# One long order for attention, soft experts and top-1 expert: phase 1 re-ordered, the tail cut into single operations, the guess taken from five experts, eight banks in one pool

## The chip, the cores and the metric

The kernel runs on one core of a Trainium2 chip. The metric is device time in microseconds (us) of a whole execution. Times are medians of runs; a profiled execution, of which the profiler keeps every instruction, is read for the reasons.

The engines are TensorE (PE, products; PEld its weight loads), VectorE (DVE), ScalarE (ACT), GpSimd (POOL) and SyncE (SP), which here only issues DMAs. Each works off its own queue in order. TensorE writes into eight PSUM banks of 128 x 512 floats; VectorE and ScalarE evict them.

## The reference

Three layers follow one another on 4608 tokens of 512 features (8 batches of 576 tokens, 8 heads of 64):

```
q_s = softmax(q, over the head's 64 features)          # per token and head
k_s = softmax(k, over the 576 tokens)                  # per feature
x   = q_s @ (k_s^T @ v)                                # attention without a score matrix

logits = x @ phi                                       # 4608 x 32, 8 experts of 4 slots
d = softmax(logits, over all tokens);  slot_input = d^T @ x
slot_out[e] = relu(slot_input[e] @ w1[e]) @ w2[e]      # 8 experts, 512 -> 1024 -> 512
x = softmax(logits, over the 32 slots) @ slot_out      # "combine"

logits2 = x @ w_gate;  e = argmax;  gate = softmax(logits2)[e] * sigmoid(x @ w_output_gate)[e]
out = gate * (relu(x @ w1_2[e]) @ w2_2[e])             # top-1 expert, 512 -> 1024 -> 512
```

All data is float32. The inputs are 28.3 MB of q, k and v, 33.6 MB of weights for the soft experts and 4.2 MB for each expert of the third layer.

## The kernel before

**Phase 1** runs over eight units `u` (a pair of batches and half of the heads each). A unit's k, q and v are loaded by `lk`, `lq`, `lv` (lines 182 to 195). On k: a maximum (`kmax`, L205), an exponential with its sum in quarters (`kexp`, L213), transposes (`ktr`, L223) and their evictions (`kev`), products with v (`kv`, L248), and the small matrices made from them. On q, in two parts: maximum (`qmax`, L318), subtraction on GpSimd (`qsub`), exponential (`qexp`), sum (`qsum`, L336, with an added epsilon and a reciprocal), multiplication on GpSimd (`qmul`), transposes (`qtr`, L357), evictions (`qev`). An eviction goes through `evac` (L199 on ScalarE for the letter `A`, L201 on VectorE for `D`). Logits come from `lg` (L377). Per pair of units an online softmax over tokens follows (`lmax` to `sc`): `su` (L419) collects slot inputs, and `sc` (L505, L506) adds them into `acc` and their denominator into `den`.

The string `ORDER` names each of these operations with its bank or home (`ktr.0.0:L1`, `kev.0.4:A,eT0`); a loop calls them in that order, and under a manual schedule each engine's queue is filled in just that order. It is the result of a search by a planner. Weights of the soft experts come in 32 pieces of 1 MB (`lw.0` to `lw.31`, four per expert: two of `w1`, two of `w2`). There are 19 homes in the on-chip memory, shared with k, q and v; `W_HOMES` gives the home of each piece. `ORDER` holds `lw.0` to `lw.16`; the others are issued by `reload` as soon as a home's last user has been called.

**The tail** has its own pools of banks (three `tp`, two `kv`, two `L`, one `U`), taken after phase 1's pool is closed (L599). It begins with the combine softmax over `l_all` (`combine_soft`, L567 to L577), the division of `acc` by `den` (L636 to L638), a transpose (L640) and its copy `sT` (L643). `SEQ` orders what follows: `i`/`j` an expert's first products (`expert_in`, L675; experts 0 to 5 do both halves in one paired pass), `t` its hidden rows transposed (L693), `o`/`p` the second products (L710), `c` a ninth of the combine weights split and transposed into `cstack` (L616, L626, L629), `m`, `d`, `n`, `r` means, distances and radii of the combine weights per batch, `G` the guess (L837 to L865): after seven experts the first token is put through the sum of these experts (`so_g`) and `w_gate`, the argmax is read into a register of SP, and that expert's weights of the third layer are loaded in eight pieces (L863, L865).

`SEQ2` orders the routing. As every token's row of x is a mix of the same 32 rows of slot outputs, a hidden unit of the guessed expert mostly has one sign for all tokens. `prep_a` and `prep_b` (L1246, L1257) form the units' values, `units` (L1259) tests each against the radii, `pack` (L1298) ranks the units that are not certain (at most 128 are kept) and selects them, `rows` (L1323) computes their row numbers and gathers their rows of `w2` by an indirect DMA (L1335) into `w2u`, `slots` (L1344) forms their mixing weights `smix`; certain units that are on are summed into one 32-row matrix `ml` (`linear_out` L1363, `linear_sum` L1371). `wsplit` (L1355, L1356) splits the gathered rows into two parts `wmh`, `wml`. `route`, `l2_tiles` (L940) and `gating` compute the second routing.

The output loop (L1427) runs over 12 groups of 3 tiles of 128 tokens. Per group `relu_part` (L1405, L1409, L1410) makes hidden rows in two parts `his`, `los`; per tile four products (L1437 with `ml`, three of L1439) and an eviction scaled by `gates` (L1442 on ScalarE, L1444 on VectorE); stores go out on SP (L1416). Groups 5 and 6 also count tokens that went to other experts (`count`, `others`); a loop over these experts (L1465) computes them with the whole 1024-unit network. It runs zero times when the guess holds for all tokens and the kept units suffice.

## Time and profile before

| | |
|---|---|
| median of 3 runs | 260.06 us (260.02 to 261.18) |
| the profiled execution | 261.23 us |
| its span, first to last instruction | 259.4 us |
| TensorE busy / VectorE / ScalarE / GpSimd | 218.4 / 157.5 / 125.5 / 93.7 us |
| mean granted clock of TensorE | 0.915 of full speed |
| read from memory / written | 66.42 / 9.44 MB |

Busy times are sums over the span; they say little of a single stage, so the rows below go by stage. The granted clock has two levels, 1.00 (2.4 GHz) and 0.50 (1.2 GHz); a mean between them is a mix of the two in time.

### The profile page before, as it was taken

How to read it: one execution, taken by the hardware profiler on the slowest of the kernel's cores; microseconds unless marked ns; L12 is line 12 of the kernel's file. 1: busy time of each engine (PE TensorE's matmuls, PEld its weight loads, DVE VectorE, ACT ScalarE, POOL GpSimd, SP SyncE). 2: the span in 40 equal slices, each digit the busy share in tenths (PEclk: the TensorE clock that was granted, in tenths of full speed). 3: DMA queues.
4: the chain of work that ended last, by engine and by line, in shares of the span. 5: the costliest groups of instructions: out<-in, count | busy, mean ns of one | idle time of the engine just before them, and what ended most of it. 6: DMA issues, size and time to landing. Idle time of an engine off the chain costs nothing. (4 is left out here: it accounts for less than half of the span.)

```text
span 259.4 us, 6248 instructions
## 1 busy us (share of the span) xinstructions
PE 218.4 (84%) x2497; PEld 155.7 (60%) x2497; DVE 157.5 (61%) x315; ACT 125.5 (48%) x276; POOL 93.7 (36%) x102
## 2 busy tenths in 40 slices
PE   0397989998999999998399997998788869999940
PEld 0285777687887777774244451574675448887830
DVE  1989898979988795623675345223631075768430
ACT  0748989889998877533110211242300134553410
POOL 4268597962797987400100532001114002000000
PEclk9999999999999999999779997999955558999995
DMA  7999999999999999799719899938501003674780
GB/s 257 400 422 388 401 366 417 373 415 365 386 311 418 417 416 413 299 418 326 282 38 414 355 423 418 410 117 350 238 0 40 0 3 121 282 286 169 303 303 9
DMA packets 13203, 76.34 MB, mean 294 GB/s; under 512 B 1712, under 2 KB 3120, under 8 KB 6128
## 3 DMA queue, kind: packets, MB, share of 16 engines
q1 hardware_dynamic: 12800, 75.50, 73.8%
q8 instruction: 23, 0.38, 0.6%
q0 software_dynamic: 80, 0.26, 0.4%
q10 hardware_dynamic: 288, 0.10, 0.2%
q14 instruction: 12, 0.10, 0.1%
HBM read 66.42 MB, written 9.44 MB: 292 GB/s over the span
## 5 line engine op out<-in xcount | busy, mean ns | idle before, releaser
L349 POOL TENSOR_TENSOR qt<-qt,qi 128x1280 f32<-128x1280 f32 (+1 forms) x14 | 29.7, 2119 | 13.3 <-DVE qi L342 5.0
L325 POOL TENSOR_TENSOR qt<-qt,qm 128x1280 f32<-128x1280 f32 (+1 forms) x14 | 29.5, 2120 | 8.3 <-DVE qm L318 8.0
L248 PE MATMUL kv<-ek,vt 128*64 128x64 f32 x512 | 21.3, 231 | 0.6 <-DMA vt<-in_v_dram 0.6
L248 PEld LDWEIGHTS kv<-ek,vt 128*64 128x64 f32 x512 | 18.3, 144 | 3.2 <-issue 2.2
L336 DVE TENSOR_REDUCE qs<-qt 128x20 f32<-128x1280 f32 (+1 forms) x14 | 18.7, 1334 | 0.6 <-ACT qt L329 0.6
L318 DVE TENSOR_REDUCE qm<-qt 128x20 f32<-128x1280 f32 (+1 forms) x14 | 18.5, 1333 | 0.0
L675 PE MATMUL kv<-we,sT 128*32 128x256 f32 (+1 forms) x288 | 16.9, 357 | 0.0
L329 ACT ACTIVATE qt<-qt 128x1280 f32<-128x1280 f32 (+1 forms) x14 | 16.4, 1169 | 1.0 <-POOL qt L325 1.0
L213 ACT ACTIVATE kt<-kt,km 128x576 f32<-128x576 f32 x20 | 15.4, 774 | 2.3 <-DVE km L205 2.3
L205 DVE TENSOR_REDUCE km<-kt 128x4 f32<-128x2304 f32 x5 | 12.7, 2532 | 4.6 <-DMA kt<-in_k_dram 4.6
L199 ACT COPY ek<-p 128x512 f32<-128x512 f32 (+1 forms) x25 | 13.1, 555 | 3.7 <-PE p L223 3.6
L223 PE MATMUL p<-ident,kt 128*128 128x128 f32 x70 | 12.5, 311 | 1.9 <-ACT ksum L269 0.8
L710 PE MATMUL U<-we,hte 128*32 128x512 f32 x88 | 12.3, 670 | 1.8 <-DVE hte L695 1.8
L357 PE MATMUL p<-ident,qt 128*128 128x128 f32 x88 | 13.2, 280 | 0.6 <-POOL qt L349 0.4
L1439 PE MATMUL kv<-mst,hr 128*128 128x512 f32 (+1 forms) x30 | 12.1, 405 | 0.7 <-ACT hr L1409 0.7
L199 ACT COPY eT<-p 128x512 f32<-128x512 f32 (+1 forms) x21 | 10.8, 532 | 3.8 <-PE p L357 3.6
L675 PEld LDWEIGHTS kv<-we,sT 128*32 128x32 f32 x288 | 9.3, 116 | 5.6 <-issue 2.4
L223 PE MATMUL L<-ident,kt 128*128 128x128 f32 x20 | 3.8, 313 | 10.4 <-ACT kt L213 9.9
L629 ACT CAST cstack<-tp 128x512 fp32r<-128x512 f32 x9 | 5.3, 587 | 14.7 <-PE tp L626 14.7
L1439 PE MATMUL L<-mst,hr 128*128 128x512 f32 (+1 forms) x30 | 11.9, 399 | 0.0
L223 PEld LDWEIGHTS p<-ident,kt 128*128 128x128 f32 x70 | 8.7, 156 | 4.7 <-ACT kt L213 1.4
L357 PEld LDWEIGHTS p<-ident,qt 128*128 128x128 f32 x88 | 9.6, 140 | 3.1 <-issue 1.9
(331 smaller groups left out, 523.1 us busy)
## 6 DMA issues: line engine op xcount, KB each, us to landing
we<-in_w_dram SPq DMA_DIRECT2D x26, 1024.0 KB, 8.6
out_dram<-ob SPq DMA_DIRECT2D x11, 768.0 KB, 3.3
...
```

The lines of the kernel that those rows point to most:

```text
L199: nc.scalar.copy(out=o, in_=i)
L213: nc.scalar.activation(out=t, in_=t, func=AF.Exp, bias=st_["km", u][:, x:x + 1], accum_out=st_["ksum", u][:, x:x + 1])
L223: nc.tensor.transpose(t[:, n * P:(n + 1) * P], ks_[u][:, j * P:(j + 1) * P], ident)
L248: nc.tensor.matmul(o[D * hh:D * hh + D, x * D:x * D + D], va, ek[:, g:g + D], start=(j == js[0]), stop=(j == js[-1]))
L318: nc.vector.tensor_reduce(out=m[:, :n], in_=t.rearrange("p (x d) -> p x d", d=D), op=ALU.max, axis=AX.X)
L325: nc.gpsimd.tensor_tensor(out=t, in0=t, in1=m.unsqueeze(2).to_broadcast([P, n, D]), op=ALU.subtract)
L329: nc.scalar.activation(out=t, in_=t, func=AF.Exp)
L336: nc.vector.tensor_reduce(out=s[:, :r, :HH], in_=t.rearrange("p (r h d) -> p r h d", h=HH, d=D), op=ALU.add, axis=AX.X)
L349: nc.gpsimd.tensor_tensor(out=t, in0=t, in1=s.unsqueeze(2).to_broadcast([P, n, D]), op=ALU.mult)
L357: nc.tensor.transpose(t[:, n * P:(n + 1) * P], qs_[u][:, o:o + P], ident)
L675: nc.tensor.matmul(hp[NS * g:NS * g + NS, o], sT[:, c, :], w, start=(c == 0), stop=(c == C - 1))
L1439: nc.tensor.matmul(op, a[:, x], w[:, d0:d1], start=False, stop=(k == 2))
```

## The change

Phase 1 has a new `ORDER` from a new search; the tail's functions are cut into named single operations too, and one string `TAIL` (with a short `LAST` behind it) gives their order, their banks, and for evictions their engine. Much of the diff is that cutting. What differs in the work:

- Unit 0's k is loaded in four pieces and its q in two, and `kmax` of unit 0 works by quarters.
- `qsum` is cut into `qsum`, `qadd` and `qrec` (the same three instructions).
- 19 weight pieces are issued in `ORDER`; `lw.19` to `lw.31` stand in `TAIL` by hand instead of through `reload`.
- One pool of eight banks (`p0 p1 p2 kv0 kv1 L0 L1 U`) serves both phases.
- `acc` is transposed without being divided by `den`; the reciprocal `rd` scales each expert's hidden rows when they are evicted (`hc`).
- The guess is made from five experts (`EG = 5`), and the other three accumulate in a bank of their own.
- Twelve dummy products (`h.n:bank` does n) stand at four places of `TAIL`.
- The units' test scales the batch means by the inverse root of the radii (a power on GpSimd) and takes a minimum over the eight batches before it squares; the selection is made by four instructions per half instead of one.
- The first products of five tiles (`AHEAD`) stand ahead of `LAST`, which holds the split of the gathered rows.
- The last stores go out on the queue of the engine that evicted them.

```
-SEQ = """i0 j0 i1 j1 t0 i2 j2 m0 o0 p0 c t1 i3 j3 m1 o1 p1 c f t2 d0 d1 i4 j4 c o2 p2 m2 t3 n0 n1 d2 d3 i5 j5 c o3 p3 t4 n2 n3
-r0 c o4 r1 p4 t5 r2 i6 j6 c o5 p5 t6 c o6 p6 G0 c G1 G2 G3 i7 c j7 c t7 c o7 p7"""
-SEQ2 = """
-a.0 a.1 b.0 a.2 b.1 u0.0 a.3 b.2 q.0 b.3 k.0 u0.1 u0.2 u1.0 r.0 l.0 k.1 r.1 u1.1 u1.2 s.0 s.1 c.0 u0.3 u1.3 g.1 4.0
-l.1 4.1 g.2 c.1 5.0 g.3 w.0 g.4
-"""
+LOOP = "kv0 L0 U kv1 L1".split()
+AHEAD = 5
+ORDER = """
+lk.0.0:k0 lq.0.0:k1 lk.0.3 lq.0.1 lk.0.1 lk.0.2 lk.1:k2 lq.1:k3 lv.0:x0 lv.1:x1 lk.3:q0 lq.2:q1 lk.2:eq0 lq.5:eq1
+kmax.0.0 kexp.0.0 qmax.0.0 ktr.0.0:p0 kev.0.0:A,eT0 kmax.0.3 qsub.0.0 qmax.0.1 kexp.0.3 ktr.0.4:p1 kmax.0.1 kev.0.4:A
...
+TAIL = """
+cs.0 xt:p0 hz.1 hz.0 zc.0 xc:A zc.2 h.4:L0 in.0:p1 rc.0 xr.0 cs.1 zc.1 xr.1 zc.3 in.2:p2 cs.2 lw.19 lw.20 hc.0:D zc.4
+zc.5 zc.6 cs.3 tr.0:L1 lw.21 lw.22 in.1:kv0 hc.2:A hr.0:D cs.4 cs.5 cs.6 o.0.0:kv1 hc.1:A in.3:U lw.23 ca.0 ft.0 me.0
...
+o.1.1 ds.3.3 lw.28 lw.29 nm.3.0 ds.2.2 nm.3.1 ct.3:L1 nm.3.2 hz.3 nm.2.0 ds.2.3 o.2.0 cc.3:D ca.5 cd.5 ct.2:p0 lw.30
+nm.2.1 ct.5:p1 nm.2.2 ca.4 cc.2:D tr.3:U tr.4:p2 cc.5:A cd.4 o.2.1 hc.5:A hr.3:D ra.0 ca.7 i.6:L1 cd.7 lw.31 hz.4
+hr.4:D o.3.0 o.3.1 j.6 hz.5 o.4.0 hc.6:D o.4.1 tr.6:p0 G.0 hz.6 ct.4:p1 hr.6:D tr.5:U G.1:kv0 ca.6 cc.4:D hr.5:A cd.6
+ct.7:p2 G.2 G.3:L1 cc.7:D ct.6:kv1 G.4 o.5.0:p0 cc.6:D ca.8 cd.8 i.7:U G.5 zc.7 o.5.1 zc.8 zc.9 zc.10 ct.8:p1 hz.7
+o.6.0 cc.8:D j.7 o.6.1 hc.7:D G.6 tr.7:kv0 ra.1:p2 hr.7:A ra.2 h.2:L0 o.7.0 ra.3 lm.0 lm.1 lm.2 lm.3 ln.0 ln.1 ln.2
+ln.3 ra.4:kv1 ra.5 o.7.1 ra.6 rc.2 sb.0 sb.1 h.5:L0 to.0:L1 zc.11 to.1 tc.0:D q.0:p1 tc.1:D h.1:L0 q.3 a.0:U q.1 q.2
+a.1:kv0 ac.0:D l.1.0:p2 ac.1:D l.0.0:kv1 b.0:p0 a.2:L1 a.3:p1 ac.2:D b.1 ac.3:D b.2:U u.0.0 u.0.1 l.0.1 u.0.8 u.0.2
+u.0.7 u.0.4 b.3 u.0.3 u.0.9 u.0.5 l.0.2 u.0.6 u.1.7 k.1.0:kv0 u.0.10 u.1.1 u.1.8 k.0.1:L1 u.0.11 u.1.0 u.1.2 l.0.3
+u.1.9 u.1.4 k.0.2 4.0:p1 k.0.3 k.0.4 k.0.5 k.0.6 u.1.3 l.0.4 u.1.5 u.1.6 s.0:p0 u.1.10 l.0.5 u.1.11 k.1.1 rw.0:U
+lc.0:D k.1.2 k.1.6 4.1 k.1.3 k.1.4 k.1.5 ga.0.0 ga.0.1 ga.0.2 rw.1 5.0:A ga.0.3 l.1.1 ga.0.4 rw.2 5.1:L1 ga.0.9 rw.3
+ga.0.5 ga.0.11 l.1.2 ga.0.13 ga.0.6 5.2 s.1 ga.0.7 l.1.3 5.3 s.2 l.1.4 ga.0.8 rl.0:kv1 rl.1:kv0 ga.0.10 l.1.5 rh.0
+ga.0.12
+"""
+LAST = """
+ga.0.14 lc.1:A rz.0 ga.0.15 w.0 rh.1 w.1 rz.1
+"""
...
-    def kmax(u):
-        m = sp.tile([P, 4], F32, tag="km", name="km", bufs=2)
+    def kmax(u, x=None):
...
+        o = slice(0, 4) if x is None else slice(x, x + 1)
         nc.vector.tensor_reduce(
-            out=m, in_=ks_[u].rearrange("p (x s) -> p x s", x=4), op=ALU.max, axis=AX.X, negate=True
+            out=st_["km", u][:, o], in_=ks_[u].rearrange("p (x s) -> p x s", x=4)[:, o], op=ALU.max, axis=AX.X,
+            negate=True,
         )
...
+    def hot(n, bk):
+        scratch = bank(bk)
         for _ in range(n):
             nc.tensor.matmul(scratch[:, :4 * VC], zero[:, :P], zero, start=True, stop=True)
...
-    nc.vector.tensor_scalar(out=acc, in0=acc, scalar1=rd, scalar2=None, op0=ALU.mult)
-    ts_ = bank("tp")
-    nc.tensor.transpose(ts_[:, :P], acc, ident)
+    def xt(bk):
+        t = bank(bk)
+        nc.tensor.transpose(t[:, :P], acc, ident)
+        sx["xt"] = t
...
+    def hc(e, eng):
+        t = sp.tile([P, FQ], F32, tag="pm", name="h_sb", bufs=3)
+        scaled(eng, t, sx.pop(("hp", e))[:, :FQ], rd)
+        sx["h", e] = t
...
+    EG = 5
...
+    def e_out(e, j, bk=None):
+        if bk:
+            sx["so", e // EG] = bank(bk)
...
+                start=(e in (0, EG) and j == 0),
+                stop=(e in (EG - 1, E - 1) and j == 1),
...
+            nc.gpsimd.tensor_tensor(out=rsq, in0=rsq, in1=mhalf, op=ALU.pow)
...
+        elif x == 3:
+            nc.vector.tensor_reduce(out=vmn[:, ks], in_=v, op=ALU.min, axis=AX.X)
...
+        elif x == 6:
+            nc.vector.tensor_tensor(out=unf[:, ks], in0=vmn[:, ks], in1=asq[:, ks], op=ALU.is_le)
...
+        else:
+            i = k0 + x - 3
+            nc.vector.tensor_scalar(
+                out=KX["gu"][:, i], in0=io1, scalar1=rkk[:, i:i + 1], scalar2=None, op0=ALU.is_equal
+            )
...
+    early = {i: bank(m) for i, m in enumerate(LOOP[:AHEAD])}
+    for i, t in early.items():
+        nc.tensor.matmul(t, cstack[:, i * P:(i + 1) * P], ml, start=True, stop=False)
+    do(LAST)
...
-                op = bank(m_tags[n % 5])[:, :d1 - d0]
+                op = early.get(i)
                 x = slice(t * P, (t + 1) * P)
-                nc.tensor.matmul(op, cstack[:, i * P:(i + 1) * P], ml[:, d0:d1], start=True, stop=False)
+                if op is None:
+                    op = bank(LOOP[n % len(LOOP)])[:, :d1 - d0]
+                    nc.tensor.matmul(op, cstack[:, i * P:(i + 1) * P], ml[:, d0:d1], start=True, stop=False)
...
-                    store_all(g, t, t + 1, d0, d1)
+                    store_all(g, t, t + 1, d0, d1, nc.scalar if eng == "A" else nc.sync)
```

In `TAIL`, `cs` is the combine softmax, `xt`/`xc`/`xr` the transpose, its copy and the reciprocal, `in`/`i`/`j` the experts' first products, `hc` their eviction, `tr`/`hr` transpose and rectifier, `o` the second products, `ca`/`cd`/`ct`/`cc` the combine weights, `G` the guess, `lm`/`ln` its loads, `sb`/`to`/`tc` the sum of the two banks of experts with transpose and copy, `q`/`l`/`lc`/`ga` the second routing, `a`/`ac`/`b`/`u` the units, `k` ranks and selection, `rw` row numbers and gather, `s` mixing weights, `4`/`5` the linear part, `w` the split of the gathered rows, `rl`/`rh`/`rz` the hidden rows of a group.

## Rows read from the trace of the kernel before

**Rows 1.** The page's strip of 40 slices: what the transfers moved.

```profile
GB/s 257 400 422 388 401 366 417 373 415 365 386 311 418 417 416 413 299 418 326 282 38 414 355 423 418 410 117 350 238 0 40 0 3 121 282 286 169 303 303 9
```

**Rows 2.** By stage: length, busy PE, PEld, DVE, ACT, POOL, clock, DMA share, GB/s.

```profile
9.87:104.00 94.13, 89.15 (x1350) 70.88 (x1352) 83.07 (x116) 80.05 (x175) 70.64 (x45) 1.00 1.00 393
104.00:126.30 22.30, 20.06 (x304) 14.20 (x300) 8.36 (x21) 8.35 (x23) 3.20 (x6) 1.00 0.88 338
...
130.70:177.30 46.60, 44.12 (x532) 21.30 (x533) 20.22 (x58) 9.93 (x24) 9.92 (x24) 0.93 0.79 317
177.30:188.20 10.90, 8.65 (x84) 6.24 (x81) 6.23 (x29) 3.48 (x12) 0.68 (x1) 1.00 0.72 290
188.20:208.70 20.50, 16.68 (x72) 11.29 (x71) 4.45 (x14) 1.66 (x4) 3.93 (x7) 0.50 0.04 13
208.70:215.40 6.70, 5.44 (x11) 3.71 (x12) 4.34 (x12) 2.50 (x6) 0.23 (x1) 0.50 0.01 2
```

**Rows 3.** The timeline at the handover: start, duration, engine, line, what; in brackets idle before.

```profile
125.90 0.35 DVE L505 SCALAR_TENSOR_TENSOR acc<-acc,w,L 128x128 f32<-128x128 f32 x1 [1.10 <-PE L L496]
...
129.34 0.28 DVE L638 TENSOR_SCALAR acc<-acc,rd 128x128 f32<-128x128 f32 x1
...
130.69 0.20 PEld L675 LDWEIGHTS kv<-we,sT 128*32 128x32 f32 x8 [0.53 <-ACT sT L643]
```

**Rows 4.** TensorE's timeline in the experts, and where it leaves them.

```profile
139.60 0.44 PE L693 MATMUL tp<-ident,h_sb 128*128 128x128 f32 x2
139.97 1.93 PE L675 MATMUL kv<-we,sT 128*32 128x256 f32 x32
...
142.25 1.92 PE L710 MATMUL U<-we,hte 128*32 128x512 f32 x16
...
146.65 0.66 PE L626 MATMUL tp<-ident,st 128*128 128x128 f32 x4
...
177.25 0.40 PE L585 MATMUL tp<-zero 128*128 128x264 bf16 x2
```

**Rows 5.** The timeline of the gather, its split, and the first output product.

```profile
193.80 1.21 POOL L1335 DMA_INDIRECT kx<-in_m2r_dram,idx  x1 [7.50 <-DVE idx L1334]
...
208.76 0.80 PE L1437 MATMUL kv<-mst,cstack 128*128 128x512 f32 x1 [0.76 <-DVE mst L1373]
...
209.19 0.60 ACT L1355 CAST mst<-kx 128x512 fp32r<-128x512 f32 x1
...
209.82 0.69 DVE L1356 TENSOR_TENSOR mst<-kx,mst 128x512 fp32r<-128x512 f32 x1
...
kx<-in_m2r_dram,idx POOLq DMA_INDIRECT x1, 3.6
```

**Rows 6.** The timeline of the output loop: two groups' hidden rows, and the last eviction.

```profile
216.83 0.34 PE L1405 MATMUL tp<-cstack,kx 128*128 128x384 f32 x1
...
219.77 0.33 PE L1405 MATMUL tp<-cstack,kx 128*128 128x384 f32 x1
...
249.43 0.48 DVE L1444 TENSOR_SCALAR ob<-L,gates 128x256 f32<-128x256 f32 x1 [0.20 <-PE L L1439]
```

**Rows 7.** The timeline at the start of phase 1.

```profile
6.31 2.55 DVE L205 TENSOR_REDUCE km<-kt 128x4 f32<-128x2304 f32 x1 [4.64 <-DMA kt<-in_k_dram]
6.36 1.28 ACT L213 ACT_TABLE_LOAD   x1 [6.36 <-DMA kt<-in_k_dram]
...
9.87 0.44 PE L223 MATMUL L<-ident,kt 128*128 128x128 f32 x1 [9.87 <-ACT kt L213]
```

**Rows 8.** VectorE's groups by line, 9.87 to 104 us: busy, mean ns, idle before.

```profile
L201 DVE COPY ek<-p 128x512 f32<-128x512 f32 x5 | 3.5, 692 | 1.7 <-PE p L223 1.7
```

**Rows 9.** The stores' line by itself: duration of an issue on SP, min/median/max in ns.

```profile
L1416 SPq DMA_DIRECT2D out_dram<-ob x15: 332/332/580, 216.9 to 250.5; - x15
```

**Rows 10.** SP's timeline: the last weight pieces and the guess's loads.

```profile
149.60 4.23 SPq L547 DMA_DIRECT2D we<-in_w_dram  x6
172.74 2.18 SPq L863 DMA_DIRECT2D vz<-in_m_dram  x4
```

More of the change, by code (lines that the diff above doesn't have):

```diff
@@ L893, in tile_attention_soft_moe_top1_moe @@
-    x = 0
-    for op in SEQ.split():
-        if op == "c":
-            combine(x)
-            x += 1
-        else:
-            steps[op[0]](*map(int, op[1:]))
-    warm(WARM[0])
-    so_sb = sp.tile([P, DM], F32, tag="U_sb", name="so_sb")
-    so7 = st_e.pop("so7")
-    for i in range(2):
-        o = slice(i * DM // 2, (i + 1) * DM // 2)
-        nc.vector.tensor_tensor(out=so_sb[:, o], in0=so7[:, o], in1=so_g[:, o], op=ALU.add)
-    cstack = st_["cstack"]
-    tso = bank("tp")
-    for c in range(C):
-        nc.tensor.matmul(
-            tso[:, c * P:(c + 1) * P], so_sb[:, c * P:(c + 1) * P], sum4.rearrange("p c s -> p (c s)"),
-            start=True, stop=True,
-        )
@@ new lines, in tile_attention_soft_moe_top1_moe, with sb, to @@
+    so_b = sp.tile([P, DM], F32, tag="so_b", name="so_b")
+    soT = sp.tile([P, C, P], F32, tag="kvT", name="soT")
+    HM = DM // 2
+    def sb(x):
+        o = slice(x * HM, (x + 1) * HM)
+        nc.vector.tensor_tensor(out=so_b[:, o], in0=sx["so", 1][:, o], in1=so_g[:, o], op=ALU.add)
+    def to(x, bk=None):
+        if bk:
+            sx["to"] = bank(bk)
+        for c in range(2 * x, 2 * x + 2):
+            nc.tensor.matmul(
+                sx["to"][:, c * P:(c + 1) * P], so_b[:, c * P:(c + 1) * P], sum4.rearrange("p c s -> p (c s)"),
+                start=True, stop=True,
+            )
@@ new lines, in tc_, with q_ @@
+    def tc_(x, eng):
+        evac(eng, soT[:, 2 * x:2 * x + 2], sx["to"][:, x * HM:(x + 1) * HM].rearrange("p (c x) -> p c x", c=2))
+    gst = late.tile([P, 2 * E], F32R, name="gst")
+    l2 = late.tile([P, NT, 2 * E], F32, name="l2")
+    def q_(x, bk=None):
+        if x in (0, 3):
+            t = sx["q"] = bank(bk) if bk else sx["q"]
+            for c in (0, 1) if x == 0 else (2, 3):
+                nc.tensor.matmul(t[:, :2 * E], soT[:, c, :], wgo[:, c, :], start=(c == 0), stop=(c == C - 1))
+        elif x == 1:
+            nc.scalar.copy(out=gst, in_=sx["q"][:, :2 * E])
+        else:
+            nc.vector.tensor_tensor(
+                out=gst[64:], in0=sx.pop("q")[64:, :2 * E], in1=gst[64:].bitcast(F32), op=ALU.subtract
+            )
@@ L980, in prep_a @@
         def prep_a(j):
[L981 removed]
+            s4 = cbank("L")
             for c in range(C):
@@ L1344, in slots @@
[L1344 to L1360 removed]
+                    r[:, i:KH], ones, unf[:, k0 + i - 1:k0 + i].to_broadcast([P, KH - i]), start=False,
@@ new lines, in s_, with w_ @@
+    def s_(x, bk=None):
+        if bk:
+            sx["s"] = bank(bk)
+        if x < 2:
+            for i in range(KH * x, KH * x + KH):
+                nc.tensor.matmul(
+                    sx["s"][:, :P], KX["tma"][:, i, 0:P], KX["gu"][:, i], start=(i == 0), stop=(i == KF - 1)
+                )
+        else:
+            nc.scalar.copy(out=KX["smix"], in_=sx.pop("s")[:, :P])
+    def w_(x):
+        if x == 0:
+            nc.scalar.copy(out=KX["wmh"], in_=KX["w2u"])
+        else:
+            nc.vector.tensor_tensor(out=KX["wml"], in0=KX["w2u"], in1=KX["wmh"].bitcast(F32), op=ALU.subtract)
@@ L1361, in linear_out, with lo_ @@
+    def lo_(h, bk=None):
+        if bk:
+            sx["m"] = bank(bk)
         for kk in range(KH * h, KH * h + KH):
@@ new lines, in tile_attention_soft_moe_top1_moe, with rl, rh @@
+    his, los, obs, hps = {}, {}, {}, {}
+    def rl(g, bk=None):
+        W = GT * P
+        t = hps[g] = bank(bk) if bk else cbank("tp")
+        nc.tensor.matmul(t[:, :W], KX["smix"], cs_[0][:, g * W:(g + 1) * W], start=True, stop=True)
+    def rh(g):
+        W = GT * P
+        if not his:
+            KX.update(hr=home("eT0", "hr", F32R), lr=home("eT1", "lr", F32R))
+        o = (g % 6) * W
+        his[g] = KX["hr"][:, o:o + W]
+        los[g] = KX["lr"][:, o:o + W]
+        nc.scalar.activation(out=his[g], in_=hps[g][:, :W], func=AF.Relu)
```

1046 lines of the change are left out of this document (517 added, 529 removed).

## The prediction

> **What bounds the kernel now.** I read the strip of 40 slices first [rows 1], then busy time by stage [rows 2], then the timeline at each place where one stage hands over to the next. TensorE is the engine to follow, and its share means something else in each stage. From the first transpose to 104 us it is busy 89.15 of 94.13 us at a granted clock of 1.00 (2.4 GHz), VectorE 83.07 and ScalarE 80.05: three engines near full, so an order can only win what lies idle. From 130.7 to 177.3 us (the eight experts) it is busy 44.12 of 46.6 us at a mean clock of 0.93 [rows 2]; the weights stream meanwhile, after a hole in which the transfers stood still (the slices at 38 and, later, 117 GB/s [rows 1]). From 188.2 to 215.4 us the clock is 0.50 (1.2 GHz) [rows 2]: latency chains with small products, and the first tiles of the output loop at half speed. That gives five terms: A phase 1, B the handover to the experts, C the experts, D routing up to the first output product, E the loop. Their boundaries are 126.25 us (last accumulation of the state, 125.90+0.35), 130.69 (first expert product) [rows 3], 177.25 (TensorE leaves the last expert for dummy products) [rows 4], 208.76 (first output product) [rows 5] and 249.43 (last eviction begins) [rows 6].
>
> **A, phase 1 (126.25 us now).** Unit 0's k and q are now loaded in pieces, and k's maximum is taken by quarters. Before, VectorE starts at 6.31 us, when all of k has landed, and reduces for 2.55; the table load (1.28) runs beside it; the first transpose comes at 9.87 [rows 7]. A quarter of 1152 KB at some 400 GB/s [rows 1] lands 2.2 us earlier (0.7 instead of 2.9) and is reduced in 0.64 us, so the table load becomes the longer arm: it ends at 6.31-2.2+1.28 = 5.4 us, and with the 1.0 us that lay between the end of the reduction (8.86) and the first transpose, TensorE starts at 6.4 us, 3.5 sooner [rows 7]. The added reductions are the old 2.55 us cut up; the four added loads take SP 0.33 to 0.58 us each in its queue [rows 9], ahead of data that needs 0.7 us a piece. Splitting the denominators into named steps adds no instruction. The rest is a permutation: every product stays, but by the letters of the two orders ten evictions go from ScalarE to VectorE (88 and 24 become 78 and 34), at 0.69 us [rows 8] 6.9 us more for VectorE, which has 11.1 us idle up to 104; most of the new ones stand in the last units, where it is busy 8.36 of 22.30 us [rows 2]. Bounds: the head and half of TensorE's 5.0 idle us, -6; the evictions uncovered less the head, +3. I take -3.0, the head without its last half microsecond.
>
> **B, handover (4.44 us now).** The state is complete at 126.25 us, but its division by the denominator waits on VectorE behind two passes of the softmax and starts at 129.34; 1.07 us after its end (129.62) the first expert product runs [rows 3]. The change transposes the state undivided and divides when each expert's hidden rows are evicted, a scale on an instruction that exists. The 1.07 us stays, 3.37 goes. Four dummy products stand on TensorE between that transpose and the first expert; two took 0.40 us [rows 4], so at most 0.8, mostly beside the copy that TensorE waits for: I charge 0.3. One pool of eight banks takes away the change of pools; the row of the first expert product waits for the copy and not for a bank [rows 3], so that counts nothing. Bounds -3.7 to -1; taken -3.1. Late next: the eviction of expert 0, which needs the reciprocal behind the same softmax passes; TensorE has experts 2 and 1 to do in between.
>
> **C, experts (46.56 us now).** Idle 2.5 us. A mean clock of 0.93 means 6.5 of 46.6 us at half speed, 3.2 us lost [rows 2]. The floor is 46.56-2.5-3.2 = 40.9; by pieces it is 8 x (0.44+1.93+1.92) for transposes and products and 9 x 0.66 for the combine weights, 40.3, with some 3 for means and guess on top and 0.07 off for each of some 43 groups that overlaps the next [rows 4]. I leave 1.7 us for waits and a cold start: 42.6, -4.0. Can the weights keep up? SP issued the last pieces by 153.8 us and they streamed until the slice that ends near 169, so the last expert could not have run before some 170 [rows 1, 10]. In the change 19 of 32 pieces are issued before the tail instead of 17, and the first expert product frees two homes 3 to 6 us sooner, which shifts that end to 163 to 166 us; C would end at 126.25-3.0+1.34+42.6 = 167.2. Both limits meet there, so I don't take the whole 5.7. The guess goes from seven experts to five and is read on SP behind the last weight. Before, its eight loads were issued from 172.74 us [rows 10], after the weights had ended; now they follow without a hole and end near 175, before their users. SP's wait for the guess holds up these loads alone. Bounds -5.5 to -1.
>
> **D, routing (31.5 us now).** The sum of the experts, its transpose and the copy stay. From 177.3 to 208.7 us TensorE is busy 8.65+16.68 = 25.3 of 31.4 us, so a closed order gains 6.1 at the same clock. The clock fell 11 us into the stage; with those 11 us full instead of 8.65 busy, 2.3 us of work moves to the full clock and saves as much again at the end [rows 2]. The chain that can't be closed: last ranks, selection, row numbers, the gather (3.6 us from issue to landing), the split of the gathered rows (0.60, and 0.69 on VectorE), loop. Before, the gather was issued at 193.80, landed near 197.4, and its split waited until 209.19 [rows 5], so it cost nothing; now it ends last together with TensorE's queue. A new wait comes with it: the five first products put ahead of the gathered rows begin with bank kv0, which group 1 of the hidden rows holds until its remainder is taken, and that instruction stands on VectorE behind the split of the gathered rows. Behind that product wait the four others, whose banks are free, and the whole loop. They start some 0.6 us after the split rather than before it: no gain counted for them and 0.9 us of loss. The units' test loses two instructions a half and the selection becomes four short ones, both in VectorE's idle time (4.45 busy of 20.5 [rows 2]). The power on GpSimd has no row; between a gate product of some 0.2 us and nothing known above, I take 0.5 and count nothing, since its result is needed only after the sum of the experts. Bounds: -13 (all at the full clock, 25.3-8.3 busy and the gather) to -2; taken -7.5.
>
> **E, loop (40.7 us now).** Three tiles take 2.94 us at the full clock (216.83 to 219.77), twelve groups 35.3 [rows 6]. Before, 6.7 us ran at half speed with 1.3 idle [rows 2]. The change too starts the loop in a cold stage: I leave 2.6, so 37.9, -2.8. Bounds -5 to 0. After the loop nothing is shortened: the last stores are shared out between SP's and ScalarE's queues, and an issue takes SP 0.33 us [rows 9].
>
> The Trainium skill ("Trainium Kernel Development and Optimization", Key Constraints) says that loads and stores of the SP, ACT and POOL queues run on the same 16 DMA engines and that several issuers save issue time alone. Rows 9 agree as far as they go; by that rule the sum would be shorter by one issue, 0.3 us, by mine by nothing, since the store before has been issued when the last eviction ends.
>
> **Sum.** -3.0-3.1-4.0-7.5-2.8 = -20.4 us. The profiled execution took 261.23 us (span 259.4 and 1.8 around it), 1.2 above the median of 260.06; from the median it is 239.7.
>
> **Rivals.**
> - Phase 1 doesn't move. For: three engines above 85% and 6.9 us more on VectorE. Against: a head start of 3.5 us that needs no cover. A becomes +3, the rest stays at -17.4: 245.7 us.
> - The gather takes the place of the closed gaps: D gains 3 and E nothing, as the loop starts cold and late behind kv0. For: the wait above. Against: TensorE's own queue behind the last selection is as long. -13.1: 247.0 us.
> - The clock stays at 1.00 through D. For: denser products and twelve dummies. Against: no dummy stands after the first step of routing, and 16.68 busy of 20.5 us left it at 0.50 [rows 2]. D gains 5 more, E 2.6: 232.1 us. The Trainium skill ("TensorE: Matmul & The Clock Gate", Why this matters for your kernels) says that gaps between bursts of products bring the clock down; by that rule this case is the one to expect if the gaps close. The fall at 188.2 us, with 8.65 of 10.9 us busy before it, speaks against it.
> - Slower: the guess of five experts misses. Then the loop over other experts runs once, 36 tiles of 24 products at 0.23 us, some 199 us more: 459 us. It decides when the largest of the first token's eight logits over five experts isn't the final one. Worked out from the reference's inputs (seed 0) it is expert 2 in both, over five with 1.0e-4 against 2.9e-5 for the next.
>
> **How the numbers follow.** Chances: my sum 0.50, phase 1 unmoved 0.17, gather 0.15, full clock 0.13, a missed guess 0.02, and 0.03 for an order that stalls by more than it gains. The half widths of the terms (4.5, 1.3, 2.3, 5.5, 2.5) add as squares to 8; with the first two rivals above and the third below, 230 to 252 us. My sum's own range is 234 to 246. 0.5% (1.3 us) is what can be told from no change. Faster 0.94, same 0.02, slower 0.04.
>
> **What would show it.** A: first transpose near 6.4 us, last accumulation of the state near 123. B: first expert product 1.1 to 1.5 us after it. C: no slice near 38 GB/s, the guess's loads issued before 165 us, 42 to 43 us from the first expert product to the last. D: 24 us, the gather's split last, the first loop product waiting for VectorE. E: a half-speed stretch reaching into the loop. A second large load of one expert's weights, or TensorE under 90% busy before 104 us, would make me wrong.

## The result, and the profile after

The changed kernel took 249.07 us in its profiled execution (span 247.3 and 1.8 around it), against 261.23 before. The median over four runs of each was 251.02 against 260.62, and the ratio is 0.953 (95% interval 0.9456 to 0.9604). Run once more on another chip it gave 249.38 (248.97 to 250.5) against 261.36, ratio 0.957 (0.9517 to 0.9623). Some executions of every kernel here are a few per cent longer at a lower mean clock; the ratios and the ranges below leave them out, and the profiled executions of two experiments (the old order, the guess from seven) are of that kind, so their traces serve for order and issue times alone.

So it is faster, as forecast, but by 12.2 us and not by 20.4 (239.7). It lies in the prediction's wide range (230 to 252), which takes in the rivals, and outside the sum's own range (234 to 246). By the prediction's boundaries, in the profiled executions:

| term | before | forecast | after | change forecast | change measured |
|---|---|---|---|---|---|
| A state complete | 126.25 | 123.2 | 129.38 | -3.0 | +3.1 |
| B from there to the first expert product | 4.44 | 1.34 | 0.78 | -3.1 | -3.7 |
| C from there to the last expert's end | 46.56 | 42.6 | 40.92 | -4.0 | -5.6 |
| D from there to the first output product | 31.5 | 24.0 | 26.88 | -7.5 | -4.6 |
| E from there to the last eviction | 40.7 | 37.9 | 41.44 | -2.8 | +0.8 |
| from there to the span's end | 9.97 | 9.97 | 7.90 | 0 | -2.1 |

The strip comes first. These are TensorE's line, the granted clock and the transfers of the changed kernel, in 40 slices of 6.2 us:

```profile
PE   0439898999979399999989998998989699999970
PEclk9999999999999869999999999999985559997995
GB/s 248 421 382 383 417 382 375 420 383 380 368 414 419 368 278 299 217 134 375 423 417 421 415 420 413 417 415 405 342 4 0 42 3 250 260 254 129 250 316 83
```

The hole that stood in the experts before [rows 1] is gone: from the 19th slice to the 28th the transfers hold 375 to 423 GB/s. But there are new marks: a 3 in TensorE's line in the 14th slice, a clock of 8 and 6 in that slice and the next, and transfers down to 134 GB/s in slices 15 to 18. The clock is at 5 in slices 31 to 33 and falls once more in the 37th slice. By stage (columns as in [rows 2]):

```profile
6.50:104.00 97.50, 82.78 (x1226) 67.83 (x1226) 84.99 (x123) 76.62 (x169) 69.45 (x43) 0.96 0.98 373
104.00:129.40 25.40, 24.33 (x428) 20.15 (x423) 13.49 (x30) 6.57 (x19) 3.88 (x5) 1.00 0.82 323
130.20:171.10 40.90, 39.73 (x535) 22.03 (x535) 25.76 (x69) 8.94 (x24) 11.04 (x30) 1.00 1.01 416
171.10:183.40 12.30, 10.30 (x106) 7.52 (x104) 6.52 (x27) 1.81 (x7) 2.58 (x4) 1.00 0.60 239
183.40:198.00 14.60, 12.40 (x54) 9.56 (x54) 6.89 (x26) 3.68 (x9) 3.39 (x6) 0.50 0.06 18
198.00:203.90 5.90, 5.90 (x14) 4.74 (x15) 1.31 (x2) 0.96 (x2) 0.00 (x0) 0.50 0.01 3
```

TensorE is busy 82.78 of 97.50 us (85%) up to 104 us; the prediction had named a share under 90% as what would make it wrong. The experts run at a mean clock of 1.00 where it was 0.93 [rows 2], with transfers at 416 GB/s instead of 317. The half-speed stretch (1.2 GHz) reaches from 183.4 into the loop.

The start went as forecast. The timeline shows VectorE's first reduction, 2.2 us sooner than in [rows 7], and TensorE's first transpose, 3.4 us sooner:

```profile
4.14 0.75 DVE L241 TENSOR_REDUCE km<-kt 128x1 f32<-128x576 f32 x1 [2.47 <-DMA kt<-in_k_dram]
...
6.49 1.08 PE L258 MATMUL p<-ident,kt 128*128 128x128 f32 x4 [6.49 <-ACT kt L248]
```

But by 20 us TensorE had lost the lead: it stood four times for ScalarE's exponentials of k, 6.75 us in all, while VectorE had next to no idle time (13.39 of 13.50 us busy):

```profile
6.50:20.00 13.50, 6.76 (x27) 5.17 (x28) 13.39 (x17) 10.32 (x22) 5.37 (x3) 1.00 1.02 400
```

The other place where phase 1 lost time, in the timeline (SP's loads, then TensorE and ScalarE; idle time before an instruction in brackets):

```profile
59.13 5.34 SPq L588 DMA_DIRECT2D we<-in_w_dram  x3
67.50 0.33 SPq L588 DMA_DIRECT2D vz<-in_w_dram  x1
72.92 0.33 SPq L225 DMA_DIRECT2D vt<-in_v_dram  x1
...
86.66 1.12 PE L283 MATMUL kv<-ek,vt 128*64 128x64 f32 x16 [4.04 <-DMA vt<-in_v_dram]
...
88.70 0.37 ACT L232 COPY eT<-p 128x256 f32<-128x256 f32 x1 [4.54 <-PE p L398]
```

and, of the two v tiles issued from 72.9 us, the time from issue to landing:

```profile
DMA to landing us min/median/max: 13.7/14.7/15.7
```

Four weight pieces (1 MB each) are issued ahead of the last two units' v and stand before it in the transfers: they landed at 75.8, 78.3, 80.8 and 83.3 us, the two v tiles at 86.6 and 90.2. The clock fell to 0.50 at 84.4 us, inside the wait, and rose again at 91.2. The kernel before has its v there first and all weights behind:

```profile
70.95 0.54 SPq L192 DMA_DIRECT2D vt<-in_v_dram  x1
...
74.02 1.02 SPq L547 DMA_DIRECT2D we<-in_w_dram  x2
```

The handover, which answers [rows 3]: the state's last accumulation, its transpose, the first expert product.

```profile
129.03 0.35 DVE L546 SCALAR_TENSOR_TENSOR acc<-acc,w,p 128x128 f32<-128x128 f32 x1 [1.05 <-PE p L537]
...
129.43 0.33 PE L666 MATMUL p<-ident,acc 128*128 128x128 f32 x1 [0.44 <-DVE acc L546]
...
130.16 1.72 PE L720 MATMUL p<-we,sT 128*32 128x256 f32 x28
```

Routing, which answers [rows 5]: the longest wait of TensorE in the first step, the gather, the last gate products, the split of the gathered rows, group 1's remainder, the first output product.

```profile
181.44 0.25 PE L1392 MATMUL kv<-unf,ones 128*128 128x4 bf16 x4 [0.76 <-DVE unf L1367]
...
189.85 1.26 POOL L1423 DMA_INDIRECT kx<-in_m2r_dram,idx  x1 [1.90 <-DVE rmx L1185]
...
195.12 0.64 PE L1000 MATMUL p<-gst,cstack 128*128 128x16 f32 x3
...
196.10 0.62 ACT L1446 CAST mst<-kx 128x512 fp32r<-128x512 f32 x1
...
197.36 0.55 DVE L1489 SCALAR_TENSOR_TENSOR lr<-kv,hr 128x384 fp32r<-128x384 f32 x1
197.96 0.79 PE L1517 MATMUL kv<-mst,cstack 128*128 128x512 f32 x1 [2.20 <-DVE lr L1489]
```

And the loop: two waits for the count of tokens of other experts, the products at half speed behind them (0.63 us instead of 0.39), the last eviction.

```profile
222.33 0.38 PE L1208 MATMUL L<-e0oh,onec 1*128 1x8 f32 x2 [0.57 <-DVE over L1207]
223.23 0.50 PE L1532 MATMUL L<-mst,cstack 128*128 128x512 f32 x1 [0.52 <-DVE fl L1211]
...
224.53 0.63 PE L1532 MATMUL U<-mst,cstack 128*128 128x512 f32 x1
...
239.40 0.48 DVE L740 TENSOR_SCALAR ob<-L,gates 128x256 f32<-128x256 f32 x1 [0.20 <-PE L L1534]
```

The first of the two waits was there before the change too; the second is new:

```profile
234.53 0.38 PE L1148 MATMUL L<-e0oh,onec 1*128 1x8 f32 x2 [0.57 <-DVE kx L1147]
```

### The profile page after: what moved, and what is told of

It reads as the page before. It is cut to its first block, busy times and chain, and to the rows that moved or that the text cites. A ratio compares the mean times of both kernels' runs of the same rounds, so it can differ in the third digit from the quotient of the medians.

```text
span 247.3 us, 6266 instructions
## 1 busy us (share of the span) xinstructions
PE 210.6 (85%) x2505; PEld 160.7 (65%) x2505; DVE 164.9 (67%) x335; ACT 116.9 (47%) x261; POOL 95.4 (39%) x104
## 5 line engine op out<-in xcount | busy, mean ns | idle before, releaser
L358 POOL TENSOR_TENSOR qt<-qt,qm 128x1280 f32<-128x1280 f32 (+1 forms) x12 | 25.2, 2119 | 12.6 <-DVE qi L376 7.1
L390 POOL TENSOR_TENSOR qt<-qt,qi 128x1280 f32<-128x1280 f32 (+1 forms) x12 | 25.3, 2120 | 12.2 <-DVE qi L384 10.4
L248 ACT ACTIVATE kt<-kt,km 128x576 f32<-128x576 f32 x24 | 18.8, 797 | 0.5 <-DVE km L241 0.5
L241 DVE TENSOR_REDUCE km<-kt 128x4 f32<-128x2304 f32 (+1 forms) x9 | 15.6, 1738 | 2.5 <-DMA kt<-in_k_dram 2.5
L351 DVE TENSOR_REDUCE qm<-qt 128x20 f32<-128x1280 f32 (+1 forms) x12 | 15.8, 1334 | 1.0 <-DMA qt<-in_q_dram 1.0
L368 DVE TENSOR_REDUCE qs<-qt 128x20 f32<-128x1280 f32 (+1 forms) x12 | 16.0, 1334 | 0.7 <-ACT qt L362 0.7
L398 PE MATMUL p<-ident,qt 128*128 128x128 f32 x76 | 11.6, 281 | 1.5 <-DVE mq L325 0.9
L1534 PE MATMUL kv<-mst,hr 128*128 128x512 f32 (+1 forms) x30 | 12.3, 411 | 0.0
L418 PE MATMUL L<-eT,mq 128*32 128x256 f32 (+1 forms) x128 | 11.1, 411 | 0.0
L460 PE MATMUL U<-qt,dz 128*32 128x256 f32 x120 | 9.9, 393 | 0.0
L358 POOL TENSOR_TENSOR vz<-vz,qm 128x1280 f32<-128x1280 f32 (+1 forms) x4 | 8.4, 2120 | 3.7 <-DVE qm L351 3.1
L390 POOL TENSOR_TENSOR vz<-vz,qi 128x1024 f32<-128x1024 f32 (+1 forms) x4 | 8.4, 2118 | 2.0 <-DVE qi L384 2.0
## 6 DMA issues: line engine op xcount, KB each, us to landing
kt<-in_k_dram SPq DMA_DIRECT2D x5, 1152.0 KB, 12.3
vz<-in_q_dram SPq DMA_DIRECT2D x2, 1152.0 KB, 12.3
```

What stands on the lines that cost most here:

```text
L241: nc.vector.tensor_reduce(out=st_["km", u][:, o], in_=ks_[u].rearrange("p (x s) -> p x s", x=4)[:, o], op=ALU.max, axis=AX.X, negate=True,)
L248: nc.scalar.activation(out=t, in_=t, func=AF.Exp, bias=st_["km", u][:, x:x + 1], accum_out=st_["ksum", u][:, x:x + 1])
L351: nc.vector.tensor_reduce(out=m[:, :n], in_=t.rearrange("p (x d) -> p x d", d=D), op=ALU.max, axis=AX.X)
L358: nc.gpsimd.tensor_tensor(out=t, in0=t, in1=m.unsqueeze(2).to_broadcast([P, n, D]), op=ALU.subtract)
L368: nc.vector.tensor_reduce(out=s[:, :r, :HH], in_=t.rearrange("p (r h d) -> p r h d", h=HH, d=D), op=ALU.add, axis=AX.X)
L390: nc.gpsimd.tensor_tensor(out=t, in0=t, in1=s.unsqueeze(2).to_broadcast([P, n, D]), op=ALU.mult)
```

## Experiments

The theory after the result: A was lost in one wait for v and the half-speed stretch behind it; D and E to the clock, to the bank kv0 and to a gap in the loop. Rival: three engines near full, or the weights, set the length anyway, and each gain is given back. All edits are to the changed kernel unless it says otherwise.

**The weights behind v.**

```diff
-... lw.1 ... lw.2 ... lw.3 ... lw.4 ... lv.7:x0 ... lv.6:x1
+... lv.7:x0 ... lv.6:x1 lw.1 lw.2 lw.3 lw.4
```

> The changed kernel with weight pieces 1 to 4 loaded after the last two units' v instead of ahead of them; nothing else moved. Theory (these 4 MB stood in the transfer queue ahead of v of units 7 and 6, whose issue at 72.9 us landed only 13.7 us later): v lands by 80 us, TensorE's 4.0 us wait for it goes, the granted clock stays 1.00 through phase 1, the state is complete at 122.5 to 125 us instead of 129.4, total 242 to 245. Rival (the weights are the limit behind it): the wait goes too, but pieces 1 to 4 and all after them land later, the experts wait for weights and take 44 to 47 us instead of 40.9: 247 to 249.

245.46 us in its profile, 243.0 to 245.46 over three runs, ratio 0.9325 (0.9266 to 0.9384). The landing time fell to a third, and TensorE ran into unit 7's products of v without a wait where it had stood for 4.04 us (0.5 us of waiting for v is left later):

```profile
DMA to landing us min/median/max: 5.5/5.7/5.9
```

```profile
81.58 1.24 PE L561 MATMUL L<-ident,ls 128*64 128x32 f32 x36
82.66 0.66 PE L283 MATMUL kv<-ek,vt 128*64 128x64 f32 x16
```

The clock stayed at 1.00 until the state was complete at 125.12 (4.3 sooner; 3.4 us at half speed followed, over the handover), and the experts took 40.44 us, not more: the theory on A holds, the rival of the weights does not. The miss is in D, 30.2 us instead of 26.9: the clock fell at 173.0, 6.2 us behind the experts' end. E was 38.6: the clock came back 3.2 us into the loop and not 5.9, and the second fall did not come.

**The old order.**

```diff
-ORDER = """ lk.0.0:k0 lq.0.0:k1 lk.0.3 ... sc.2 ute.3 sa.3:p1 sc.3 """
+ORDER = """ lk.0:k0 lq.0:k1 lv.0:x0 ... (before's, with qadd and qrec behind each qsum) ... sc.3 lw.17 lw.18 """
```

> The changed kernel with the order of phase 1 (and the first 19 weight homes) of the kernel before; the tail is the new one. Theory (the new order loses its head start in one wait for the last units' v, 82.6 to 86.7 us, and in the 6.8 us at half speed behind it): the last accumulation of the state ends near 126 us as in the kernel before instead of 129.4, no half-speed stretch in phase 1, and the tail keeps its lengths: 245 to 246.5 us against 249.1 for the changed kernel. Rival (the new tail is short only because the new order has 19 weight pieces under way early): phase 1 ends at 126 but the experts take 43 to 45 us instead of 40.9: 247 to 249. If phase 1 still ends at 129, the one pool of banks or something else in the set-up is the cause and not the order.

242.87 to 246.23 us, ratio 0.9345 (0.9288 to 0.9403): the new tail behind the old phase 1 is 4 to 5 us faster than the change as made. There is no wait for v; the last accumulation ends at 126.26 (125.91+0.35):

```profile
125.91 0.35 DVE L543 SCALAR_TENSOR_TENSOR acc<-acc,w,L 128x128 f32<-128x128 f32 x1 [1.27 <-PE L L534]
```

So the new order of phase 1 made the kernel slower, and by as much as the repair above wins back. In the last run below the old order has the state complete at 125.77.

**The head alone**, in the kernel before.

```diff
-lk.0:k0 lq.0:k1 lv.0:x0 ... kmax.0 kexp.0.0 qmax.0.0 kexp.0.3
+lk.0.0:k0 lq.0.0:k1 lk.0.3 lk.0.2 lq.0.1 lk.0.1 lv.0:x0 ... kmax.0.0 kexp.0.0 qmax.0.0 kmax.0.3 kexp.0.3
```

> The kernel before with one edit: unit 0's k and q loaded in pieces and k's maximum taken by quarters. Theory of the prediction (TensorE's head start needs no cover): first transpose at 6.5 us instead of 9.87 and the state complete 2 to 3.4 us sooner than 126.25: 257 to 258.5 us against 260.1 to 260.6. Rival (by 20 us TensorE had done 6.8 us of work in the changed kernel against 8.8 before, although it began 3.4 us sooner, so what follows is set by other engines): first transpose at 6.5 as well, state complete within 0.7 us of 126.25, time within 0.7 us of before.

259.14 to 262.46 us over eight runs, ratio 0.9983 (0.9937 to 1.003): no difference that can be told. TensorE began 3.6 us sooner, and by 20 us nothing was left of it: 8.85 us of work against 8.82 in the kernel before. The state was complete at 126.10 (125.75+0.35), 0.15 sooner.

```profile
6.23 1.09 PE L237 MATMUL L<-ident,kt 128*128 128x128 f32 x4 [6.23 <-ACT kt L227]
...
125.75 0.35 DVE L517 SCALAR_TENSOR_TENSOR acc<-acc,w,L 128x128 f32<-128x128 f32 x1 [1.11 <-PE L L508]
```

```profile
0.00:20.00 20.00, 8.85 (x112) 7.21 (x114) 14.31 (x22) 8.19 (x15) 8.75 (x15) 1.00 0.92 360
```

The rival holds.

**A free bank for group 1.**

```diff
-rl.0:kv1 rl.1:kv0
+rl.0:kv1 rl.1:p1
```

> The changed kernel with the hidden rows of group 1 in bank p1 instead of kv0, so that the five first products of the loop no longer stand behind the remainder of group 1. Theory (that wait is the 2.2 us idle ahead of the first output product at 197.96): the first output product starts at 195.8 to 196.2, the five products (2.1 us at half speed) are done before the gathered rows are split at 197.4, the first product with gathered rows comes near 197.5 instead of 200.26, and the time falls by 2 to 2.7 us to 246.4 to 247.1. Rival (the gathered rows and the half-speed clock set the start): the five products move, but the loop reaches the full clock no sooner, or the rows' split is late behind ScalarE: less than 1 us gained, 248.2 to 249.1.

244.43 to 246.28 us, ratio 0.9367 (0.9314 to 0.942), some 4 us less than the change; the profiled spans differ by 2.9. The five first products run in the old gap, and the first with gathered rows comes 27.0 us behind the experts' end (171.16) instead of 29.2:

```profile
195.92 0.77 PE L1517 MATMUL kv<-mst,cstack 128*128 128x512 f32 x1
...
198.20 0.63 PE L1534 MATMUL kv<-mst,hr 128*128 128x512 f32 x1
```

The theory holds, with a little more than the 2 to 2.7 us that it had forecast; the first product with gathered rows came 0.7 us later than it said.

**More dummy products, and none.**

```diff
-to.1 tc.0:D q.0:p1 ... b.0:p0 ... k.1.0:kv0 ... 4.0:p1 ... rw.0:U
+to.1 tc.0:D h.5:L0 q.0:p1 ... h.2:L0 b.0:p0 ... h.7:L0 k.1.0:kv0 ... h.2:L0 4.0:p1 ... h.4:L0 rw.0:U
 (and h.2 or h.4 ahead of l.0.1, l.0.3, l.0.4, l.0.5: 32 products in all)
```

> The changed kernel with 32 further dummy products in routing, where TensorE waits or runs small products (ahead of the second step's weights, the first half's rows, four gate steps and the row numbers). Theory (the clock falls because TensorE does too little in the 12.3 us behind the experts, 10.4 us of them busy): no fall before the loop, TensorE's queue in routing shrinks from 12.4 to some 8 us with the dummies and the loop's first 5.9 us run at full speed: 243 to 245.5. Rival (the clock falls all the same): 32 dummies at 0.11 us at full and 0.2 at half speed lie in TensorE's queue, which is the bound there: 3 to 5 us more, 251.5 to 254.

240.56 to 243.05 us, ratio 0.933 (0.9258 to 0.9402). The clock held at 1.00 until 191.8, 23.0 us behind the experts' end and not 12.3, though the added products lie in TensorE's own queue:

```profile
168.80:181.10 12.30, 11.59 (x123) 8.77 (x121) 6.37 (x27) 1.91 (x7) 2.58 (x4) 1.00 0.65 258
181.10:191.60 10.50, 8.53 (x70) 6.47 (x66) 6.37 (x26) 3.55 (x9) 3.39 (x6) 1.00 0.09 27
191.60:195.10 3.50, 2.69 (x6) 2.17 (x7) 0.76 (x2) 0.00 (x0) 0.00 (x0) 0.53 0.00 0
```

In the first 12.3 us TensorE was busy 11.59 instead of 10.30. D took 23.6 (-3.3) and E 38.5 (-3.0); the rest of the 8.6 us between the profiled spans lies ahead of the edit, in A and C. Of E's 3.0 us, some 1.6 are a shorter stretch at half speed at the start of the loop (2.8 us instead of 5.9); the rest is the second fall, which did not come here although its two waits stood, so it cannot be put down to the dummies. The forecast of no fall at all missed: the clock fell inside the 2.8 us wait ahead of the loop.

```diff
-h.4:L0 ... h.2:L0 ... h.5:L0 ... h.1:L0
+...
```

> The changed kernel without its twelve dummy products (four at the handover to the experts, two ahead of the last expert product, six in the first step of routing). Theory (they keep TensorE's clock up): the half-speed stretch that begins at 183.4 us begins 6 to 10 us earlier, near 174 to 177, as it did in the run with the weights behind v; 3 to 5 us lost: 250 to 252. Rival (they only fill time that is idle anyway, since with all of them in place that other run fell to half speed 6.3 us after the last expert product): fall within 2 us of 183.4 relative to the end of the experts, time within 1 us of the changed kernel's 247.9 to 249.1.

248.65, 248.97 and 251.38 us, ratio 0.9587 (0.9484 to 0.9691): the time can't be told from the change, as the rival had it, but the clock fell at 174.4, 6.0 us behind the end of the last expert product (168.40) and not 12.3, as the theory had it.

```profile
168.40:174.40 6.00, 4.09 (x40) 3.29 (x41) 2.77 (x10) 0.17 (x1) 0.80 (x1) 1.00 1.03 410
174.40:198.60 24.20, 22.02 (x111) 16.09 (x110) 10.74 (x42) 5.41 (x15) 5.14 (x9) 0.50 0.11 39
```

D was 3.4 us longer; E was 2.9 shorter, because in this execution the clock came back 3.1 us into the loop and the second fall did not come, with the same two waits. Neither reading wins alone.

**The count of other experts in its own bank.**

```diff
-        cp = cbank("L")
+        cp = cbank("tp")
         nc.tensor.matmul(cp[:, 2 * E:2 * E + 1], onec, cnt1, start=True, stop=True)
+        nc.tensor.matmul(cp[:, E:2 * E], onec[0:1, :], e0oh, start=True, stop=True)
         nc.vector.tensor_scalar(out=over, ...)
-        nc.tensor.matmul(cp[:, E:2 * E], onec[0:1, :], e0oh, start=True, stop=True)
```

> The changed kernel with the count of other experts in a bank of the hidden rows instead of one of the loop's, and its third product ahead of the comparison it does not need. Theory (the loop's two waits of 0.57 and 0.52 us at 221.8 to 223.2 are for VectorE's steps of that count, and the 3.4 us at half speed from 224.35 come from this gap): both waits go, the clock stays 1.00 from 204 us to the end of the loop, 2.3 to 2.8 us gained: 245.3 to 246.8. Rival (the half-speed stretch has another cause): only the idle 1.1 us goes: 246.8 to 248.

245.69 to 246.49 us, ratio 0.9431 (0.9341 to 0.952). Both waits are gone, the clock stays at 1.00 from 204 us on, and E falls from 41.44 to 38.69 us, the forecast 2.8, with the same cold start of the loop as in the change:

```profile
221.56 0.38 PE L1207 MATMUL p<-e0oh,onec 1*128 1x8 f32 x2
221.88 0.50 PE L1532 MATMUL L<-mst,cstack 128*128 128x512 f32 x1
```

1.1 us of it are the waits. The rest is the fall that did not come; as it also stayed away in three profiles that kept the waits, this one profile does not show by itself that the edit prevents it. The time, at least 2.5 us below every run of the repeat, fits.

**The guess from seven experts.**

```diff
-    EG = 5
+    EG = 7
-... G.0 ... G.5 ... o.5.0:p0 ... o.6.1 hc.7:D G.6 ... o.7.0
+... o.5.0 ... o.6.1 hc.7:D G.0 ... G.5 ... o.7.0:p0 ... G.6
```

> The changed kernel with the guess made from seven experts' sum (as before the change) instead of five. Theory of the prediction (the earlier guess lets its eight loads follow the weights without a hole): the loads are issued from 168 to 169 us instead of 163.4, a hole of 1 to 3 us opens in the transfers, the first step of routing waits for its weights, 1 to 3 us lost: 249 to 252. Rival (hidden anyway, since weights still fill the queue until some 168 us): the loads come later but the products that need them do not wait, time within 0.7 us of the changed kernel's 247.9 to 249.1.

248.19, 251.18 and 251.9 us, ratio 0.9597 (0.9501 to 0.9693). The loads are issued from 171.05 us and not 163.36, and a hole opens in the transfers, but the median of 251.2 stands 1.8 us above the repeat's 249.38 on the same chip, with intervals of the ratios that overlap: inconclusive. That the guess from five is worth more than 2 us is not borne out.

**The last stores on one queue.**

```diff
-store_all(g, t, t + 1, d0, d1, nc.scalar if eng == "A" else nc.sync)
+store_all(g, t, t + 1, d0, d1)
```

> The changed kernel with the last group's stores all on SP's queue, as before the change. Theory (two queues end the last transfers sooner): the time from the last eviction to the end of the span is 9.5 to 10 us as in the kernel before, instead of 7.9: 1.6 to 2.1 us more. Rival (the end does not hang on who issues; the run without dummies had 9.83 with both queues): 7.8 to 8.3 us or, at random, 9.8; the time within 0.7 us of the changed kernel run beside it.

247.31 to 249.06 us, ratio 0.9522 (0.9462 to 0.9582). From the last eviction to the end of the span (245.6) it is 7.84 us, as with both queues (7.90):

```profile
237.76 0.48 DVE L740 TENSOR_SCALAR ob<-L,gates 128x256 f32<-128x256 f32 x1 [0.20 <-PE L L1534]
```

The rival holds: the second queue buys nothing. The run beside it was the changed kernel itself:

> The changed kernel once more, unaltered, on the chip of this call, so that the other runs have it beside them. Every theory expects 247.9 to 249.1 us and a profile with the wait for v of some 4 us at 82.6 us, a half-speed stretch behind it, a second one from 10 to 13 us after the experts' end, and 0.6 and 0.5 us idle in the loop.

It came out nearly as expected (248.97 to 250.5 us against 247.9 to 249.1), with a wait for v of 3.8 us, the fall in routing 12.4 us behind the experts' end and the fall in the loop. One thing differed: the clock was at half speed over the handover, and B took 1.34 us, not 0.78.

```profile
129.00:132.40 3.40, 2.96 (x22) 1.46 (x26) 3.26 (x9) 0.33 (x2) 1.79 (x11) 0.50 1.03 422
```

**All four repairs at once** (weights behind v, bank p1, 32 dummies, the count's bank).

> Four edits of the earlier runs at once in the changed kernel: weight pieces 1 to 4 behind v, group 1 in bank p1, 32 dummy products in routing, the count of other experts in its own bank. Theory (four separate causes: the wait for v, the bank, the clock in routing, the gap in the loop): the state is complete near 124 to 125 us, no half-speed stretch between the experts and the loop, first product with gathered rows 22 to 23 us after the experts' end, loop 36.5 to 37.5: 231 to 236 us. Rival (the gains stand in one queue and replace each other; with the weights behind v the clock fell 6.3 us after the experts already): at most the best of them again, 239 to 243.

233.22, 233.24, 233.64 and 236.27 us, ratio 0.8983 (0.8897 to 0.907), against 249.38 for the change on the same chip. State complete at 124.53, D 20.7, E 36.7; the first product with gathered rows comes 22.5 us behind the experts' end:

```profile
166.10:186.80 20.70, 19.96 (x190) 15.17 (x188) 11.33 (x47) 3.75 (x13) 5.75 (x9) 1.00 0.41 155
186.80:223.50 36.70, 36.41 (x166) 29.57 (x165) 25.65 (x60) 18.54 (x35) 1.89 (x5) 1.00 0.58 231
```

```profile
187.99 0.50 PE L1517 MATMUL kv<-mst,cstack 128*128 128x512 f32 x1 [0.27 <-DVE lr L1489]
```

The clock is 1.00 from 127.7 us, early in the experts, to the end of the loop, and of the 2.20 us wait ahead of it 0.27 is left. Between the profiles the four edits gained 3.6, 2.8, 8.5 and 3.0 us singly, 17.9 together; at once they gain 15.9. So the gains add for the most part, and the rival falls.

**The same with the old order of phase 1** (its edit as above).

> The combined kernel of the run before, but with the old order of phase 1 and its first 19 weight homes in place of the new order with the weights behind v; bank p1, the 32 dummy products and the count's bank stay. Theory (once its wait for v is gone, the new order of phase 1 and its head start are worth the 1.1 us by which that state was complete sooner, 125.12 against 126.26): state complete near 126.2, 234 to 235.5 us against 233.2 to 233.6. Rival (the order of phase 1 is worth nothing beside the old one, since three engines near full set its length): within 0.5 us of 233.4 or below.

233.07 to 235.35 us over six runs, ratio 0.897 (0.8934 to 0.9007); the profiled spans of the two are equal at 231.3 us. The state was complete at 125.77, 1.2 later, and the experts took 39.3 us instead of 40.2. The rival holds in time: what the new phase 1 wins at its end, the next stages give back. Part of that is the clock: the run with the new order had 3.4 us at half speed over the handover (124.3 to 127.7) and this one none, and such a stretch came and went between two runs of the changed kernel too. Both versions beat the kernel before and the change.

## Why the prediction was right and wrong

**Sign and size.** The gains of B, C and D carried it: -13.9 us measured, -14.6 forecast. That their sum comes so close is luck in part: C gave 1.6 more than forecast and D 2.9 less. The time lies nearer to the two slower rivals (245.7 and 247.0) than to the sum, and neither is right in its cause, as shown below. The guess of five experts hit, as worked out: a miss would have cost some 199 us, by the prediction's estimate.

**A failed, by 6.1 us.** The step was "The rest is a permutation: every product stays". I counted which weight pieces are issued earlier, as a gain for C, and not what they are issued ahead of: of the 19 pieces put ahead of the tail, five stand in SP's order ahead of v of units 7 and 6, and four of them were still in transfer when that v was issued. Its landing went from 6.3 (the piece issued at 70.95 before) to 13.7 us and more, TensorE, ScalarE and VectorE all waited (4.0, 4.5 and 4.7 us), and 6.8 us ran at half speed; moving those four gave 4.3 us back in A. (Three other profiles with this phase 1 had 3.4 us at half speed, and the state was complete at 127.9 to 128.2.) The second error is "the head start of 3.5 us that needs no cover". It came (6.49 us) and is worth nothing: alone it changes the time by 0.998 (0.994 to 1.003), as in the first 20 us VectorE's reductions and ScalarE's exponentials set the pace. The rival "phase 1 doesn't move" had the right size, +3, but its cause, the ten evictions moved to VectorE, was not what held phase 1: with them in place and the four pieces moved, the state was complete 1.1 us sooner than before the change. What the evictions cost by themselves no run shows.

**B and C were right in mechanism and too small.** The transpose of the undivided state saves the wait behind the softmax: 0.78 us, and 1.34 in the repeat, where the clock was at half speed; the forecast was 1.34. No run takes this step back by itself, so it rests on the timeline. The experts ran with no hole in the transfers, as argued, at a clock of 1.00, and of the 1.7 us that I left for waits and a cold start little came: 40.92 us. In the experiments whose profiles can be compared they took 39.3 to 41.2 us. The one run on a cause of C, the guess from seven experts, could not decide.

**D: the bank was seen and undersized.** The wait of the first output product for group 1's remainder was named as what the trace would show, and stood there: 2.20 us, priced at 0.9. The price left out that the five products could have run in that time and that the loop's start is at half speed; the free bank gained 2.9 us between the profiles. The clock was the other half. I had it fall 11 us into the stage, it fell after 12.3, and 14.6 us ran at half speed before the loop. The rival "the clock stays at 1.00" was wrong for the twelve dummies as placed and near right on what is to be had: with 32 more D is 3.3 us and E 3.0 us shorter, and in both runs with all four repairs the clock did not fall in routing at all. The argument against it, the fall behind 8.65 busy of 10.9 us [rows 2], was carried over to a fuller stretch that no row had shown. The rival of the gather named a gain of 3 us for D and E together, and 3.8 came, but the gather was not what held them: its rows landed near 193.5 us (3.6 after the issue), and their split began at 196.10, behind ScalarE's work on the hidden rows.

The Trainium skill ("TensorE: Matmul & The Clock Gate", Why this matters for your kernels) lays the fall to gaps between bursts of products. The filled run agrees with its direction; but the longest gap ahead of the fall at 183.4 was 0.76 us, so here the clock fell behind a row of short waits and small products with no long gap.

**E failed, by 3.6 us.** I left 2.6 us for a cold start; 5.9 us ran at half speed before the clock came back, which costs half of that, some 3 us, so that term was nearly right. What the sum had at nothing are the waits for the count of other experts: one of 0.57 us, which stood in the kernel before as well, and a new one of 0.52, as the count now stands in a bank that the next tile of the loop needs. They are 1.1 us idle, and 3.4 us ran at half speed behind them in this execution, another 1.7. With both waits taken away E was 2.75 us shorter.

**After the loop** 2.1 us were gained that I had at nothing. Sharing the stores between two queues was not the cause (7.84 us with one). By the Trainium skill ("Trainium Kernel Development and Optimization", Key Constraints) a second issuer saves issue time alone, and the run agrees. The run without dummies, with the same stores, took 9.83 (247.0-237.17), the kernel before 9.97, all other profiles with the new tail 7.8 to 8.1. What sets this end stays open.

**The clock's fall in routing is not fully explained.** With the same products behind the experts it fell after 12.3 us, in the repeat after 12.4, and with the weights behind v after 6.2. No run here tells why.
